# Products of zeros on TensorE in front of ten steps of the start of an attention and MLP kernel

## The chip, the cores and the metric

The kernel runs on one core of one Trainium2 chip. A core has TensorE (PE, matrix products into PSUM), VectorE (DVE), ScalarE (ACT), GpSimd (POOL) and SyncE (SP, which issues most DMAs). Each engine takes its own instructions strictly in order and waits on semaphores for the others. The metric is the device time of one execution in microseconds; lower is better.

## The reference

The inputs are q, k, v of shape (4, 8, 576, 64) in float32 and the weights of two dense blocks. What is computed, cut to what matters:

```python
q_d, k_d, v_d = (t.reshape(B, H, Sd, 4, D).mean(axis=3) for t in (q, k, v))
out_d = sm_attn(q_d, k_d, v_d)                       # softmax attention over 144 pooled positions
out_up = np.repeat(out_d, 4, axis=2)
mask = np.abs(pos[:, None] - pos[None, :]) < 4       # local attention, 7 keys wide
attn = softmax(np.where(mask, scale * q @ k.T, -1e9))
x = (out_up + attn @ v).transpose(0, 2, 1, 3).reshape(2304, 512)
x = ((x @ w_a) * (x @ w_b)) @ w_out                  # 512 -> 1536 -> 512
h = x @ w_in                                         # 512 -> 1024
solu = h * softmax(h)
out = layernorm(solu) * g_ln @ w_out2                # 1024 -> 512
```

## The kernel before, in words

The 2304 tokens are four batches of 576. The dense part works through five blocks of tokens (four of 512, one of 256). Each block runs through 12 chunks of the 1536 middle columns: `emit_A` makes the two products ab of a chunk (n = 0 for w_a, n = 1 for w_b), `emit_a` and `emit_mult` multiply them, `emit_p` splits the result into a high and a low part, and `emit_B` multiplies with w_out. Every float32 matrix is split into a high and a low part (xTh, xTl; a weight is a pair), and three products replace one. Weight tiles come through DMA as raw words; ACT (L109, L110), DVE (L114, L117), ACT (L123) and DVE (L130) turn each into such a pair.

Ahead of the first chunk the attention for the first 512 tokens has to be made. It has two parts, in small plain float32 products on TensorE.

- Pooled attention, for each of the four pairs of heads hp of batch 0: `qsum` (DVE L200, sums q and k over four positions into qkds), `scores` (PE L223, tile S), `smax` (DVE L233), `exps` (ACT L246, tile E), `norm` (DVE, POOL L255), `ptr` (PE transposes L266, tile PT), `pte` (ACT copy L272, PTs), `pvm` (PE L283, tile pv: 16 products of 144 columns), `pve` (ACT L289, tile up).
- Local attention, for each of the four strips s of 128 tokens: `scores` (PE L353, tile lS), `mask` (DVE L364, lP), `smax` (DVE L370, L371), `exps` (ACT L374), `norm` (DVE L380, POOL L383), `ptr` in two halves (PE transposes L393, tile lPT), `pte` (ACT copies L401, lPTs), `pvm` in two halves (PE L412, tile lo), `evac` (DVE L424, tile lx, adds up, which needs all four pairs), `split` (ACT L441 into xTh, then DVE or POOL L442 into xTl).

The first chunk then runs in halves of 256 columns: n = 0 and n = 1 on the first two strips, then n = 0 and n = 1 on the last two (L473, 12 products of 256 columns each). From the second chunk on, products have 512 columns.

The order on each engine is written out by hand: a table of times per step (L650 to L670) is sorted, the steps are emitted in that order, and no scheduler changes it. The SP queue is in the same table: the q and k tiles of the four pairs, the v tiles, then weight tiles and v strips by turns. ACT prepares weight tiles between attention steps: behind the copy of the first half of strip 0 stands L109 and L110 of its third weight tile, and behind these the copy L401 of strip 0's second half.

PSUM has two buffers tagged "ab" (PT, lPT of strips 0 and 1, then ab), acc0 and acc1 (S of odd pairs, lS of strip 2, later sums), x0 and x1 (pv, lo, lPT of strips 2 and 3, lS of strip 0 and from 4 on) and S.

A float32 product stands as two records in the profile's rows: the 16 products of pv are "x32" there. A transpose is one record, and so is a product of the split parts.

Of the kernel before, what the change touches and what calls it, by code (L numbers as in the profile page):

```python
# [7 lines left out]
F32 = mybir.dt.float32  # L8
# [20 lines left out]
EDGES = [8, 9, 13, 17]  # L29
NBOOT = NSUB  # L30
PT = [0, 16, 17]

QW, KW = 64, 70
TILES = [(t // 9, 64 * (t % 9), min(max(64 * (t % 9) - 3, 0), S - KW), 0, QW, 0) for t in range(NT // QW)]
# [4 lines left out]
def kernel(  # L39
# [98 lines left out]
    W1 = {}  # L138
    W2 = {}


    att = ExitStack()
    pool_p = att.enter_context(tc.tile_pool(name="pooled", bufs=1))
# [42 lines left out]
    def pooled_items(b, hp):  # L186
        i = b * NP + hp
        st = {}

        def room():  # L190

            if "room" not in st:
                st["room"] = slot(12 + hp, F32, (128, 1024), "E")
            return st["room"]

        def qsum(n):
            def f():
                if n == 0:
                    st["qk"] = pool_p.tile([128, 2, SD], F32, tag="qkds", name="qkds")
                DVE.tensor_reduce(out=st["qk"][:, n, :], in_=qkr[i][n].rearrange("p (c t) -> p c t", t=4),  # L200
                                  axis=AX.X, op=ALU.add)
            return f

        def vsum(kh):
            def f():
                if kh == 0:
                    st["v"] = pool_p.tile([72, 2, 2 * D], F32, tag="vds", name="vds")
                t = vr[i][:, kh, :].rearrange("p (t c) -> p t c", t=4)
                POOL.tensor_tensor(out=t[:, 0:2], in0=t[:, 0:2], in1=t[:, 2:4], op=ALU.add)
                POOL.tensor_tensor(out=st["v"][:, kh, :], in0=t[:, 0], in1=t[:, 1], op=ALU.add)  # L210
            return f

        def scores():
            if b:
                st["S"] = [aps.tile([72, 2 * SD], F32, tag=f"x{e}", name="S") for e in range(2)]
            elif hp % 2 == 0:
                t = aps.tile([72, 2, 512], F32, tag="S", name="S")
                st["S"] = [t[:, e, 0:2 * SD] for e in range(2)]
            else:
                st["S"] = [ps.tile([72, 512], F32, tag=f"acc{e}", name="S")[:, 0:2 * SD] for e in range(2)]  # L220
            for half in range(2):
                for e in range(2):
                    PE.matmul(  # L223
                        out=st["S"][e][:, half * SD:(half + 1) * SD],
                        lhsT=st["qk"][e * 64:e * 64 + 64, 0, half * 72:half * 72 + 72],
                        rhs=st["qk"][e * 64:e * 64 + 64, 1, :], start=True, stop=True,
                    )

        def smax():
            sv = [t.rearrange("p (h k) -> p h k", h=2) for t in st["S"]]  # L230
            mm = pool_p.tile([72, 2, 2], F32, tag="pm", bufs=2, name="pm")
            for e in range(2):
                DVE.tensor_reduce(out=mm[:, e, :], in_=sv[e], axis=AX.X, op=ALU.max)  # L233
            DVE.tensor_scalar(out=mm, in0=mm, scalar1=-scale / 16.0, scalar2=None, op0=ALU.mult)
            st["sv"], st["mm"] = sv, mm

        def exps():
            sv, mm = st["sv"], st["mm"]
            if b:
                st["E"] = pool_p.tile([72, 2, 2, SD], F32, tag="E", name="E")  # L240
            else:
                st["E"] = room()[:72, 0:4 * SD].rearrange("p (e h k) -> p e h k", e=2, h=2)
            st["ss"] = pool_p.tile([72, 4, 1], F32, tag="ss", bufs=2, name="ss")
            for e in range(2):
                for h in range(2):
                    ACT.activation(out=st["E"][:, e, h, :], in_=sv[e][:, h, :], func=AF.Exp,  # L246
                                   bias=mm[:, e, h:h + 1], scale=scale / 16.0,
                                   accum_out=st["ss"][:, 2 * e + h, :])

        def norm():  # L250
            ss = st["ss"].rearrange("p a o -> p (a o)")
            DVE.tensor_scalar(out=ss, in0=ss, scalar1=1e-9, scalar2=None, op0=ALU.add)
            DVE.reciprocal(out=ss, in_=ss)  # L253
            ev = st["E"].rearrange("p e h k -> p (e h) k")
            POOL.tensor_tensor(out=ev, in0=ev, in1=st["ss"].to_broadcast([72, 4, SD]), op=ALU.mult)  # L255

        def ptr():
            if b:
                st["PT"] = [aps.tile([72, 2 * SD], F32, tag=f"x{e}", name="PT") for e in range(2)]
            else:  # L260
                st["PT"] = [ps.tile([72, 512], F32, tag="ab", bufs=2, name="PT")[:, 0:2 * SD] for e in range(2)]
            for e in range(2):
                for kh in range(2):
                    for h in range(2):
                        o = kh * SD + h * 72
                        PE.transpose(st["PT"][e][:, o:o + 72], st["E"][:, e, h, kh * 72:kh * 72 + 72],  # L266
                                     id_sb[:72, :72])

        def pte():
            st["PTs"] = pool_p.tile([72, 2, 2, SD], F32, tag="PTs", name="PTs")  # L270
            for e in range(2):
                ACT.copy(out=st["PTs"][:, e].rearrange("p h k -> p (h k)"), in_=st["PT"][e])  # L272

        def pvm():
            st["pv"] = aps.tile([128, SD], F32, tag="x0", name="pv")
            if b:
                v = [st["v"][:, kh] for kh in range(2)]
            else:

                v = [vr[i][:, kh, 2 * D * t:2 * D * t + 2 * D] for kh in range(2) for t in range(4)]  # L280
            for n, vt in enumerate(v):
                for e in range(2):
                    PE.matmul(out=st["pv"][e * 64:e * 64 + 64, :], lhsT=vt[:, e * 64:e * 64 + 64],  # L283
                              rhs=st["PTs"][:, e, n * 2 // len(v), :], start=(n == 0), stop=(n == len(v) - 1))

        def pve():
            if b not in up:
                up[b] = pool_p.tile([128, NP, SD], F32, tag="up", bufs=2, name="up")
            ACT.activation(out=up[b][:, hp, :], in_=st["pv"], func=AF.Copy, scale=0.25)  # L289

        return dict(load=lambda: (load_qkr(i), load_v(i)), qsum0=qsum(0), qsum1=qsum(1), scores=scores,
                    vsum=lambda: (vsum(0)(), vsum(1)()), smax=smax, exps=exps, norm=norm, ptr=ptr, pte=pte,
                    pvm=pvm, pve=pve)

# [29 lines left out]
    def local_items(s):  # L324

        st = {}
# [13 lines left out]
        def scores(hps=range(NP)):  # L340
            if hps[0] == 0:
                if s in (1, 3):
                    t = aps.tile([128, 2, 512], F32, tag="S", name="lS")
                    st["S"] = [t[:, e] for e in range(2)]
                elif s == 2:
                    st["S"] = [ps.tile([128, 512], F32, tag=f"acc{e}", name="lS") for e in range(2)]
                else:
                    st["S"] = [aps.tile([128, 512], F32, tag=f"x{e}", name="lS") for e in range(2)]
            for hp in hps:
                for n in range(2):  # L350
                    for e in range(2):
                        q, k = qk_of(n, hp, e)
                        PE.matmul(out=st["S"][e][n * QW:n * QW + QW, hp * KW:hp * KW + KW], lhsT=q, rhs=k,  # L353
                                  start=True, stop=True, skip_group_check=True)
# [30 lines left out]
        def ptr(half):  # L385
            def f():
                if s < 2:
                    pt_ = ps.tile([KW, 4, 128], F32, tag="ab", bufs=2, name="lPT")
                else:
                    pt_ = aps.tile([KW, 4, 128], F32, tag=f"x{half}", name="lPT")  # L390
                for a in range(4):
                    hp, e = 2 * half + a // 2, a % 2
                    PE.transpose(pt_[:, a, :], st["P"][:, NP * e + hp, :], id_sb)  # L393
# [10 lines left out]
        def pvm(half):  # L404
            def f():
                if half == 0:
                    st["o"] = aps.tile([128, NP, 128], F32, tag="x1" if s < 2 else "x0", name="lo")
                for hp in (2 * half, 2 * half + 1):
                    for n in range(2):
                        for e in range(2):  # L410
# [49 lines left out]
    def emit_A(blk, j, n, c0, c1):  # L460

        xh, xl = xT_of(blk)
        if (blk, j) not in abs_:
            if width[blk] == WIDE:
                abs_[blk, j] = [ps.tile([128, WIDE], F32, tag="ab", bufs=2, name="ab") for _ in range(2)]
            else:
                t = ps.tile([128, 2, 256], F32, tag="ab", bufs=2, name="ab")
                abs_[blk, j] = [t[:, n_, :] for n_ in range(2)]
        wh, wl = W1[3 * j + n]
        for k in range(4):  # L470
            ws = slice(k * 128, k * 128 + 128)
# [247 lines left out]

    mhalf = base.tile([128, 1], F32, name="mhalf")  # L720
    DVE.memset(mhalf, -0.5)
    warm = base.tile([128, 1], F32, name="warm")
    ACT.activation(out=warm, in_=mhalf, func=AF.Exp)

# [145 lines left out]
```

## Time and profile before

| what | before |
|---|---|
| median of three runs | 805.21 us (800.87 to 806.71) |
| the profiled execution's own time | 803.08 us |
| its span, first to last instruction | 801.3 us |
| TensorE busy | 765.4 us (96%) |
| DVE, ACT, POOL busy | 376.9, 332.5, 228.5 us |
| chain of work that ended last | PE 81%, DVE 7%, ACT 5%, DMA 3% |
| largest chain lines | PE ab L473 33%, PE o L616 13%, PE h L548 11% |

The profile is of one execution. Rows of a timeline merge instructions of one kind that follow each other: start, length, engine, line, operation, output and inputs, count, and in brackets how long the engine stood idle before and what it waited for. "PEclk" is the clock that TensorE was granted, as a share of 2.4 GHz. The ends of products are modelled, so a row overlaps the start of the next by some hundredths of a microsecond. All times of rows count from the start of the span.

### The profile page before, as it was taken

To read this page: it belongs to the slowest core of one execution; us is meant where nothing else is said; L and a number is where in the kernel's file an instruction comes from. 1 tells how busy PE (TensorE), PEld (TensorE's weight loads), DVE (VectorE), ACT (ScalarE), POOL (GpSimd) and SP (SyncE) were. 2 spreads that over 40 slices of the span, in tenths; PEclk is the share of its full clock that TensorE was granted. 3 is DMA by queue.
4 is the path that set the end of the run, shared out by engine and by line. 5 is a ranking of instruction groups with operands and counts; after the bars stand their busy time and mean duration, and the time that the engine had idled before them with its cause. 6 is when DMAs were issued, how large, how long until landed. Compare 5 with 4: busy or idle time off the path is not lost.

```text
span 801.3 us, 12378 instructions
## 1 busy us (share of the span) xinstructions
PE 765.4 (96%) x4848; PEld 621.3 (78%) x4848; DVE 376.9 (47%) x689; ACT 332.5 (41%) x691; POOL 228.5 (29%) x204
## 2 busy tenths in 40 slices
PE   4979999998999999999999999999899999999997
PEld 3867777776787787777787888888788888888885
DVE  5678889974223324223213220126765373545441
ACT  3648777653222324322323221147645343344432
POOL 1242343431322222232111121114222352334320
PEclk9979999999999999999999999999999999999999
DMA  8977844214212203111102000036422554444321
GB/s 239 239 259 246 268 152 137 70 30 139 59 57 61 83 30 110 59 52 34 42 15 80 15 27 1 0 112 208 155 79 66 157 173 144 145 134 145 103 79 40
DMA packets 65226, 85.04 MB, mean 106 GB/s; under 512 B 9016, under 2 KB 46136, under 8 KB 65168
## 3 DMA queue, kind: packets, MB, share of 16 engines
q1 hardware_dynamic: 64864, 84.02, 33.8%
q8 instruction: 38, 0.62, 0.3%
q10 hardware_dynamic: 304, 0.23, 0.1%
q14 instruction: 20, 0.16, 0.1%
HBM read 66.93 MB, written 17.30 MB: 105 GB/s over the span
## 4 chain that ended last, share of the span: by engine, by line
PE 81%; DVE 7%; ACT 5%; DMA 3%; issue 3%; POOL 1%; SPq 0%; DVEq 0%; ACTq 0%; POOLq 0%
PE ab L473 33%; PE o L616 13%; PE h L548 11%; PE acc L507 8%; PE accS L507 7%; PE lo L412 2%; PE pv L283 2%; PE lPT L393 2%; DVE wm L117 2%; DMA qkr<-qkp 1%; PE lS L353 1%; PE S L223 1%; DMA raw<-w 1%; PE PT L266 1%; ACT o L514 1%
## 5 line engine op out<-in xcount | busy, mean ns | idle before, releaser
L473 PE MATMUL ab<-xTh,w 128*128 128x512 f32 (+1 forms) x976 | 298.0, 375 | 6.2 <-DVE a L483 3.6
L473 PEld LDWEIGHTS ab<-xTh,w 128*128 128x128 f32 x976 | 179.9, 191 | 43.7 <-DVE a L483 5.6
L473 PE MATMUL ab<-xTl,w 128*128 128x512 f32 (+1 forms) x488 | 180.2, 369 | 0.9 <-DVE xTl L167 0.5
L490 POOL TENSOR_TENSOR pl<-a,ph 128x512 fp32r<-128x512 f32 (+1 forms) x60 | 75.1, 1251 | 234.6 <-ACT ph L489 234.6
L483 DVE TENSOR_TENSOR a<-a,ab 128x512 f32<-128x512 f32 (+1 forms) x60 | 38.0, 632 | 181.3 <-PE ab L473 181.3
L473 PEld LDWEIGHTS ab<-xTl,w 128*128 128x128 f32 x488 | 93.4, 191 | 15.1 <-DVE xTl L167 0.9
L548 PE MATMUL h<-w,o1w 128*128 128x512 f32 x432 | 103.9, 391 | 1.1 <-ACT w L123 0.9
L548 PEld LDWEIGHTS h<-w,o1w 128*128 128x128 f32 x432 | 80.1, 188 | 18.1 <-ACT w L123 1.1
L616 PE MATMUL o<-w,cTh 128*128 128x512 f32 x288 | 91.0, 397 | 1.2 <-ACT cTh L606 0.9
L507 PE MATMUL acc<-ph,w 128*128 128x512 f32 (+1 forms) x288 | 90.2, 365 | 0.0
L478 ACT COPY a<-ab 128x512 f32<-128x512 f32 (+1 forms) x60 | 32.5, 542 | 108.9 <-PE ab L473 103.7
L507 PE MATMUL accS<-ph,w 128*128 128x512 f32 x192 | 68.0, 391 | 4.2 <-ACT o L514 4.2
L616 PEld LDWEIGHTS o<-w,cTh 128*128 128x128 f32 x288 | 54.0, 188 | 14.3 <-ACT cTh L606 1.1
L489 ACT CAST ph<-a 128x512 fp32r<-128x512 f32 (+1 forms) x60 | 34.6, 577 | 67.2 <-DVE a L483 67.2
L507 PEld LDWEIGHTS acc<-ph,w 128*128 128x128 f32 x288 | 52.2, 189 | 9.1 <-issue 1.2
L616 PE MATMUL o<-w,cTl 128*128 128x512 f32 x144 | 57.2, 397 | 0.1
L507 PE MATMUL acc<-pl,w 128*128 128x512 f32 (+1 forms) x144 | 51.1, 358 | 0.1
L600 POOL TENSOR_TENSOR cTl<-raw,cTh 128x1024 fp32r<-128x1024 f32 x15 | 36.0, 2401 | 44.2 <-ACT cTh L599 36.6
L507 PEld LDWEIGHTS accS<-ph,w 128*128 128x128 f32 x192 | 36.0, 188 | 13.1 <-ACT o L514 5.5
L117 DVE CUSTOM_DVE_ANT_0 wm<-raw,wm 128x1024 uint16<-128x1024 uint16 x52 | 43.4, 845 | 2.3
L255 POOL TENSOR_TENSOR E<-E,ss 72x576 f32<-72x576 f32 x16 | 19.3, 1206 | 81.1 <-DVE ss L253 53.4
L557 DVE TENSOR_REDUCE mx<-h 128x1 f32<-128x1024 f32 x18 | 22.0, 1223 | 43.1 <-PE h L548 43.1
(91 smaller groups left out, 1005.5 us busy)
## 6 DMA issues: line engine op xcount, KB each, us to landing
raw<-w SPq DMA_DIRECT2D x52, 512.0 KB
qkr<-qkp SPq DMA_DIRECT2D x32, 288.0 KB
vd<-v SPq DMA_DIRECT2D x15, 512.0 KB
raw<-vd SPq DMA_DIRECT2D x60, 128.0 KB
vw<-vwin SPq DMA_DIRECT2D x36, 140.0 KB
vp<-vp SPq DMA_DIRECT2D x16, 288.0 KB
o1r<-o1d SPq DMA_DIRECT2D x18, 256.0 KB
out<-ob SPq DMA_DIRECT2D x18, 256.0 KB
```

What stands on the lines that cost most here:

```text
L117: DVE.tensor_tensor(out=st["w"], in0=st["w"], in1=st["low"], op=ALU.add)
L255: POOL.tensor_tensor(out=ev, in0=ev, in1=st["ss"].to_broadcast([72, 4, SD]), op=ALU.mult)
L473: PE.matmul(out=abs_[blk, j][n][:, c0:c1], lhsT=w[:, ws], rhs=x[:, k, c0:c1], start=(k == 0 and i == 0), stop=(k == 3 and i == 2), skip_gr ...
L478: ACT.copy(out=a, in_=abs_[blk, j][0])
L483: DVE.tensor_tensor(out=a, in0=a, in1=pb, op=ALU.mult)
L489: ACT.copy(out=ph, in_=a)
L490: POOL.tensor_tensor(out=pl, in0=a, in1=f32(ph), op=ALU.subtract)
L507: PE.matmul(out=accs[blk][m], lhsT=wt[:, ms], rhs=x, start=(j == 0 and i == 0 and (w == WIDE or m % 2 == 0)), stop=(j == NCH - 1 and i == ...
L548: PE.matmul(out=h[:, n * 512:n * 512 + 512], lhsT=x[:, ks], rhs=w, start=(k == 0 and q_ == 0), stop=(k == 3 and q_ == 2))
L557: DVE.tensor_reduce(out=mx, in_=st["h"], axis=AX.X, op=ALU.max)
L600: POOL.tensor_tensor(out=h4(lo), in0=raw, in1=f32(h4(hi)), op=ALU.subtract)
L616: PE.matmul(out=o, lhsT=x[:, k, :], rhs=w, start=(k == 0 and q_ == 0), stop=(k == 7 and q_ == 2))
```

## The change

A tile `zz` of 128 by 128 zeros is made by POOL at the start. A new helper `fill(key, out)` issues as many products of zeros by zeros on TensorE as the table `FILL` has under that key, 72 in all. They write into a part of the PSUM tile that the step behind them is about to use (before it does), or into a tile `fz` on acc1. Calls stand ahead of the scores, the transposes, the lo products and the first ab of a block; only the ten keys of the table have products.

```diff
--- before.py
+++ after.py
@@ -29,6 +29,8 @@
 EDGES = [8, 9, 13, 17]
 NBOOT = NSUB
 PT = [0, 16, 17]
+
+FILL = dict(lS0_0=12, lS0_1=9, lS0_3=6, PT0=5, S3=7, lPT0_0=6, lo1_0=10, lPT2_1=6, A0_256=7, lS4_0=4)
 
 QW, KW = 64, 70
 TILES = [(t // 9, 64 * (t % 9), min(max(64 * (t % 9) - 3, 0), S - KW), 0, QW, 0) for t in range(NT // QW)]
@@ -138,6 +140,18 @@
     W1 = {}
     W2 = {}
 
+    zz = base.tile([128, 128], F32, name="zz")
+
+    fz = []
+
+    def fill(key, out):
+        for _ in range(FILL.get(key, 0)):
+            if out is None:
+                if not fz:
+                    fz.append(ps.tile([128, 512], F32, tag="acc1", name="fz"))
+                out = fz[0][:, 0:128]
+            PE.matmul(out=out, lhsT=zz[:, 0:out.shape[0]], rhs=zz, start=True, stop=True, skip_group_check=True)
+
 
     att = ExitStack()
     pool_p = att.enter_context(tc.tile_pool(name="pooled", bufs=1))
@@ -218,6 +232,8 @@
                 st["S"] = [t[:, e, 0:2 * SD] for e in range(2)]
             else:
                 st["S"] = [ps.tile([72, 512], F32, tag=f"acc{e}", name="S")[:, 0:2 * SD] for e in range(2)]
+            if not b:
+                fill(f"S{hp}", st["S"][0][:, 0:128])
             for half in range(2):
                 for e in range(2):
                     PE.matmul(
@@ -259,6 +275,8 @@
                 st["PT"] = [aps.tile([72, 2 * SD], F32, tag=f"x{e}", name="PT") for e in range(2)]
             else:
                 st["PT"] = [ps.tile([72, 512], F32, tag="ab", bufs=2, name="PT")[:, 0:2 * SD] for e in range(2)]
+            if not b:
+                fill(f"PT{hp}", st["PT"][0][:, 0:128])
             for e in range(2):
                 for kh in range(2):
                     for h in range(2):
@@ -346,6 +364,7 @@
                     st["S"] = [ps.tile([128, 512], F32, tag=f"acc{e}", name="lS") for e in range(2)]
                 else:
                     st["S"] = [aps.tile([128, 512], F32, tag=f"x{e}", name="lS") for e in range(2)]
+            fill(f"lS{s}_{hps[0]}", None if s > 3 else st["S"][1][:, 384:512])
             for hp in hps:
                 for n in range(2):
                     for e in range(2):
@@ -388,6 +407,7 @@
                     pt_ = ps.tile([KW, 4, 128], F32, tag="ab", bufs=2, name="lPT")
                 else:
                     pt_ = aps.tile([KW, 4, 128], F32, tag=f"x{half}", name="lPT")
+                fill(f"lPT{s}_{half}", None if s > 1 else pt_[:, 0, :])
                 for a in range(4):
                     hp, e = 2 * half + a // 2, a % 2
                     PE.transpose(pt_[:, a, :], st["P"][:, NP * e + hp, :], id_sb)
@@ -405,6 +425,7 @@
             def f():
                 if half == 0:
                     st["o"] = aps.tile([128, NP, 128], F32, tag="x1" if s < 2 else "x0", name="lo")
+                fill(f"lo{s}_{half}", None)
                 for hp in (2 * half, 2 * half + 1):
                     for n in range(2):
                         for e in range(2):
@@ -466,6 +487,8 @@
             else:
                 t = ps.tile([128, 2, 256], F32, tag="ab", bufs=2, name="ab")
                 abs_[blk, j] = [t[:, n_, :] for n_ in range(2)]
+        if (blk, j) == (0, 0):
+            fill(f"A{n}_{c0}", None)
         wh, wl = W1[3 * j + n]
         for k in range(4):
             ws = slice(k * 128, k * 128 + 128)
@@ -719,6 +742,7 @@
 
     mhalf = base.tile([128, 1], F32, name="mhalf")
     DVE.memset(mhalf, -0.5)
+    POOL.memset(zz, 0.0)
     warm = base.tile([128, 1], F32, name="warm")
     ACT.activation(out=warm, in_=mhalf, func=AF.Exp)
 
```

Each key is a step: lS0_0, lS0_1 and lS0_3 are the scores of strip 0 for pairs 0, 1 and 3; PT0 the transposes of pair 0; S3 the pooled scores of pair 3; lPT0_0 the first half of strip 0's transposes; lo1_0 the lo products of strip 1; lPT2_1 the second half of strip 2's transposes; A0_256 the first product of the first chunk on the last two strips; lS4_0 the scores of strip 4, which belongs to the next block.

TensorE's order, from its first instruction to the pooled scores of pair 3. Before:

```order
L353 MATMUL lS<-qkr 64x70 x4
L223 MATMUL S<-qkds 72x144 x4
L353 MATMUL lS<-qkr 64x70 x4
L223 MATMUL S<-qkds 72x144 x4
L353 MATMUL lS<-qkr 64x70 x8
L223 MATMUL S<-qkds 72x144 x4
L266 MATMUL PT<-id_sb,E 72x72 x8
L223 MATMUL S<-qkds 72x144 x4
L283 MATMUL pv<-PTs,vp 64x144 x16
```

After (line numbers are those of the changed file):

```order
L153 MATMUL lS<-zz 128x128 x12
L372 MATMUL lS<-qkr 64x70 x4
L239 MATMUL S<-qkds 72x144 x4
L153 MATMUL lS<-zz 128x128 x9
L372 MATMUL lS<-qkr 64x70 x4
L239 MATMUL S<-qkds 72x144 x4
L372 MATMUL lS<-qkr 64x70 x4
L153 MATMUL lS<-zz 128x128 x6
L372 MATMUL lS<-qkr 64x70 x4
L239 MATMUL S<-qkds 72x144 x4
L153 MATMUL PT<-zz 72x128 x5
L284 MATMUL PT<-id_sb,E 72x72 x8
```

Behind the last of these rows come seven products of zeros, then the scores S of pair 3. Nothing of before has changed its place against its neighbours.

TensorE's order further on, from the scores of strip 3 to the lo products of strip 2. Before:

```order
L353 MATMUL lS<-qkr 64x70 x16
L393 MATMUL lPT<-id_sb,lP 70x128 x4
L283 MATMUL pv<-PTs,vp 64x144 x16
L393 MATMUL lPT<-id_sb,lP 70x128 x4
L266 MATMUL PT<-id_sb,E 72x72 x8
L412 MATMUL lo<-lPTs,vw 64x64 x8
L393 MATMUL lPT<-id_sb,lP 70x128 x8
L412 MATMUL lo<-lPTs,vw 64x64 x8
L283 MATMUL pv<-PTs,vp 64x144 x16
L412 MATMUL lo<-lPTs,vw 64x64 x16
L393 MATMUL lPT<-id_sb,lP 70x128 x8
L412 MATMUL lo<-lPTs,vw 64x64 x16
```

After, from the first half of strip 0's transposes:

```order
L153 MATMUL lPT<-zz 70x128 x6
L413 MATMUL lPT<-id_sb,lP 70x128 x4
L301 MATMUL pv<-PTs,vp 64x144 x16
L413 MATMUL lPT<-id_sb,lP 70x128 x4
L284 MATMUL PT<-id_sb,E 72x72 x8
L433 MATMUL lo<-lPTs,vw 64x64 x8
L413 MATMUL lPT<-id_sb,lP 70x128 x8
L433 MATMUL lo<-lPTs,vw 64x64 x8
L301 MATMUL pv<-PTs,vp 64x144 x16
L153 MATMUL fz<-zz 128x128 x10
L433 MATMUL lo<-lPTs,vw 64x64 x16
L413 MATMUL lPT<-id_sb,lP 70x128 x4
```

Behind that come six products of zeros, the other four transposes of strip 2 and its lo products. Between the six ahead of lPT and the ten behind pv of pair 3 none is added. The orders of DVE, ACT and SP are as before; POOL's has one row more, the memset of zz, ahead of its first use by the attention.

## Rows read from the trace of the kernel before

**Rows 1.** Busy time by stretch: start:end length, engines, PEclk, DMA share, GB/s

```profile
20.00:27.60 7.60, 7.60 (x109) 6.87 (x107) 2.16 (x6) 3.74 (x12) 0.27 (x1) 1.00 0.94 216
27.80:41.30 13.50, 11.33 (x188) 9.56 (x184) 12.73 (x25) 10.04 (x21) 5.01 (x5) 1.00 0.95 251
41.40:51.50 10.10, 8.37 (x83) 7.12 (x84) 8.88 (x14) 5.68 (x10) 5.14 (x4) 0.50 0.71 260
51.70:58.30 6.60, 4.72 (x61) 4.28 (x60) 3.24 (x5) 2.81 (x5) 3.14 (x5) 1.00 0.65 232
58.50:61.80 3.30, 3.30 (x18) 2.71 (x18) 2.30 (x7) 0.62 (x1) 0.00 (x0) 0.50 1.03 416
64.60:801.30 736.70, 718.80 (x4280) 582.50 (x4280) 333.75 (x605) 299.70 (x602) 211.96 (x185) 1.00 0.30 93
```

**Rows 2.** Timeline of TensorE, 13 to 34 us

```profile
13.31 0.51 PE L353 MATMUL lS<-qkr 64*64 64x70 f32 x8 [1.40 <-DMA qkr<-qkp]
13.76 1.24 PE L223 MATMUL S<-qkds 64*72 64x144 f32 x8
...
19.38 4.40 PE L283 MATMUL pv<-PTs,vp 72*64 72x144 f32 x32 [1.53 <-ACT PTs L272]
23.71 1.18 PE L266 MATMUL PT<-id_sb,E 72*72 72x72 f32 x8
24.82 2.15 PE L353 MATMUL lS<-qkr 64*64 64x70 f32 x64
26.90 2.55 PE L283 MATMUL pv<-PTs,vp 72*64 72x144 f32 x32
29.38 0.69 PE L266 MATMUL PT<-id_sb,E 72*72 72x72 f32 x8
30.00 0.72 PE L353 MATMUL lS<-qkr 64*64 64x70 f32 x32
31.49 0.63 PE L393 MATMUL lPT<-id_sb,lP 128*70 128x128 f32 x4 [0.77 <-POOL lP L383]
32.05 2.18 PE L283 MATMUL pv<-PTs,vp 72*64 72x144 f32 x32
```

**Rows 3.** Timeline of ACT around its third weight tile

```profile
33.17 0.71 ACT L109 ACTIVATE raw<-raw 128x512 f32<-128x512 f32 x1 [0.43 <-DMA raw<-w]
...
34.83 0.58 ACT L401 COPY lPTs<-lPT 70x512 f32<-70x512 f32 x1 [0.37 <-PE lPT L393]
```

**Rows 4.** Timeline of TensorE, 35 to 85 us

```profile
35.46 0.45 PE L266 MATMUL PT<-id_sb,E 72*72 72x72 f32 x4 [0.42 <-ACT lPTs L401]
...
36.46 1.07 PE L393 MATMUL lPT<-id_sb,lP 128*70 128x128 f32 x8
...
38.21 2.18 PE L283 MATMUL pv<-PTs,vp 72*64 72x144 f32 x32
42.98 1.97 PE L412 MATMUL lo<-lPTs,vw 70*64 70x64 f32 x32 [2.58 <-DVE lx L424]
...
54.11 1.15 PE L412 MATMUL lo<-lPTs,vw 70*64 70x64 f32 x32
56.71 0.39 PE L473 MATMUL ab<-xTh,w 128*128 128x256 f32 x1 [1.45 <-ACT xTh L441]
...
84.88 0.71 PE L223 MATMUL S<-qkds 64*72 64x144 f32 x8
```

**Rows 5.** Chain of work that ended last, in order of time, 42 to 70 us

```profile
42.32 0.61 DVE lx L424
...
49.15 2.73 PE ab L473 x12
...
52.75 1.43 PE ab L473 x12
...
57.53 1.96 PE ab L473 x11
...
64.61 5.74 PE ab L473 x24
```

## The prediction, before the changed kernel was run

> **What bounds the kernel now.** I read the views in this order: granted clock and busy time by stretch, the PE, ACT and DVE timelines of the first 65 us with what ended each wait, and the chain of work that ended last. From 64.6 us on TensorE is busy for 718.80 of 736.70 us [rows 1], and a chain row there starts the second chunk at 64.61 [rows 5]. So what the change gains or loses by 64.61 is what the kernel gains or loses, and all else is about those 65 us.
>
> There the reader is to see two things. First, the clock. The row for 20 to 27.6 us says 1.00, but the 32 pv records at 19.38 took 4.40 us and the same 32 at 32.05 took 2.18 [rows 2]: TensorE ran at 1.2 GHz until about 27.7, and the record of the clock just starts later. After that it is 2.4 GHz to 41.3, 1.2 to 51.5, 2.4 to 58.3, 1.2 to 61.8, then 2.4 [rows 1]. Second, in this stretch TensorE is often not what ends the wait: at 13.31 it waited for q and k, at 31.49 for POOL, at 35.46 for an ACT copy, at 42.98 for DVE, at 56.71 for ACT [rows 2, 4].
>
> **The change, part by part.** It adds one memset on POOL, ahead of anything that POOL is waited for, and 72 products of 128 by 128 zeros in TensorE's order; all other rows of all engines keep their order. No f32 product over the whole array stands in the trace. From below: pv makes 16 products of 144 columns in 2.18 us, 0.136 each, so 0.12 for 128 columns. From above: pv fills half of the array's columns with each product and two can run side by side, so 0.24 alone. I take 0.23 at 2.4 GHz, since a zero product fills the array, and 0.46 at 1.2.
>
> *Up to 13.31 us* 27 zero products run where TensorE waits for q and k; hidden. If the clock is at 2.4 GHz from there on, this becomes shorter on TensorE: S 1.24 to 0.71 (0.53) [rows 2, 4], pv of pair 0 4.40 to 2.18 (2.22), PT 1.18 to 0.69 (0.49), 64 lS records 2.15 to twice 0.72 (0.71), pv of pair 1 2.55 to 2.18 (0.37) [rows 2]: 4.3 us. Against it stand 18 zero products: five ahead of the first PT (in what the shorter S leaves), seven ahead of S3 (1.6 us against the 1.53 that pv waited at 19.38), six ahead of lPT (1.4 against 0.77): 0.5 us. TensorE comes to 35.04 about 3.8 us early.
>
> *This doesn't pass.* ACT's third L109 started at 33.17, after 0.43 us of waiting for its weight tile to land [rows 3]. Nothing in the change touches the SP queue, so it starts then again, and everything behind it in ACT's order waits. The copy L401 behind it had waited 0.37 for TensorE at 34.83: it comes 0.37 earlier, and that is the whole gain at this gate. The transposes PT of pair 3 wait for this copy (35.46, 0.42 idle) [rows 4], so they start at 35.09, and TensorE's idle time ahead of them grows to 0.42 + 3.8 - 0.37 = **3.85 us**. None of the zero products stands in this hole.
>
> *What the clock does there.* Before both falls in the trace TensorE had stood idle for less: the fall at 41.3 came about a microsecond into the 2.58 us ahead of lo at 42.98, and that at 58.4 right after 1.45 us ahead of ab at 56.71 and 0.43 more behind it (56.71 + 0.39 to 57.53) [rows 1, 4, 5]. So I take it to fall in the hole. It did not rise during the 4.40 us of pv at 19.38, which had no gap [rows 2]; PT, lo, lPT, lo and pv, which come after the hole, are work of that kind. At 2.4 GHz they took from 35.46 to 40.39 (0.45, the lo, 1.07, lo, 2.18) [rows 4]. At 1.2: half of 1.18, half of 1.97, twice 1.07, half of 1.97, 4.40, together 9.1, less 0.3 for overlapping ends: 8.8, so to 43.9. DVE's lx (42.32 before [rows 5]) needs that pv and moves too.
>
> *The ten zero products behind pv*, which would fill the 2.58 us wait, now start at 43.9 and cost between 2.3 (clock up at once) and 4.6; I take 4.0, for the clock comes up late: 47.9. Then lo 1.15 [rows 4], 49.05; lx 0.61 [rows 5], beside it half an lPT (0.55) and six zero products (1.4), 51.0; the other half 0.55, L401 0.58 [rows 3], half of lo 0.58: 52.7. Before, this point was 49.15: **3.55 late**. From here on the clock is at 2.4: ab 2.73 to 1.43 (1.30 back); then from 51.88 to 57.53 copies, transposes and lo as before, 5.6 us, with seven zero products in the 1.45 + 0.43 of waiting; the next ab 1.96 for 11 to 1.31 (0.65 back) [rows 5], S 1.24 to 0.71 (0.53 back). The wait behind that is DVE and ACT work of the same length. Four zero products (0.9) lie beside it. Sum: 3.55 - 1.30 - 0.65 - 0.53 = +1.1.
>
> The profiled execution took 803.08 us, so **804.1**, I say 804. With the ten at 2.3 it is 802.4, at 4.6 it is 804.8. The median of the runs shown is 2.1 above the profiled one, so the time can come out that much higher.
>
> If every slow piece on the path came back whole, it would be 4.3 and, further on, 0.82 (lo, 1.97 to 1.15), 1.30, 0.65, 0.53: 7.6 us. The Trainium skill (TensorE: Matmul & The Clock Gate, Part 1) says that the cost of coming up to the full clock is under 1% of a typical kernel's span, here 8.0 us: by that bound too, a gain of over 1% is all but out, though for this kernel rows and page come close to it.
>
> **Rivals.**
> *The clock holds through the hole*, or comes up too late for the hole to open. For it: gaps of 0.42 and 0.77 us did no harm in 27.8 to 41.3 [rows 1, 2, 4]. Against: 3.85 is longer than the gaps at both falls. Then 0.37 (gate), 0.82 (lo ahead of 49.15), 1.30, 0.65 and 0.53 all come back: 3.7, **799.4**.
> *The gate is none*: the tile lands earlier, and 7.6 comes back: **795.5**. Against: L109 waited for this landing, with the DMA share at 0.95 around it [rows 1, 3].
> *Zero products don't bring the clock up.* Each costs 0.46. The 18 ahead of the gate take 8.3 us against 0.53 + 1.53 + 0.77 of waits, 5.5 late, of which 0.4 is hidden by ACT's wait; the ten 4.6 against 2.58 (2.0), the seven 3.2 against 1.9 (1.3); of the six (2.8) and the four (1.8) I take 0.7 as hidden, since no wait of that length stands there (3.9). That is 12.3 late: **815.4**. It decides from 0.26 us a product on, where ten outlast 2.58 us. For it: no row shows a product of zeros. Against: the rows show nothing by which values matter. The Trainium skill (same page, Part 1) has the clock gate watch how busy the engine is, and names zeros only for another limiter, one that needs three busy cores; no run here shows either.
> *A second fall* further on, in the waits at 56 or 60, adds up to 2 us to the forecast: 806.
>
> **How the numbers follow.** The hole and its fall: 0.48 (802.4 to 804.8). The clock holds: 0.36 (799.4). Zeros don't count: 0.07. No gate: 0.05. A second fall: 0.04. The likeliest gives 804. The range takes in the first two and the last, and the 2.1 between profile and median: 798.5 to 807, which leaves out the 0.12 of the outer two and some of the spread. About 1% is what a measurement of this kernel can tell from no change, 8 us: faster by that needs the missing gate, 0.04; slower needs zeros that don't count, 0.07; the rest, 0.89, lies within.
>
> **What would show it.** In the changed profile: pv of pair 0 takes 2.2 us (if 4.4, the clock did not rise). ACT's third L109 still starts near 33.2, now with about 4 us of idle ahead. TensorE idles 3 to 4 us ahead of PT of pair 3, and pv behind it takes 4.4 (if 2.2, the clock held and the time is near 799). The ten zero products take 2.3 to 4.6. The first ab starts near 52.7, or near 48 by the first rival. The forecast is wrong if the third weight tile lands earlier or if the clock reads 2.4 GHz from 28 us on.

## The result, and the profile after

The changed kernel takes 799.84 us (median of 20 executions, 795.28 to 805.80), the kernel before 807.56 beside it (20, 800.73 to 812.54): ratio 0.992, interval 0.989 to 0.995. That is a gain of 0.8%, inside the 1% within which the prediction called a difference none, and the median lies inside the predicted range, 4 us below the predicted 804. The two profiled executions, 803.08 and 799.16 us, differ by 3.9, the medians by 7.7. This factor of two is the subject of much of what follows. The ratio is worked out from the executions of both kernels and is not the ratio of the two medians.

Of the profile after, busy time by stretch (start:end length, PE, PEld, DVE, ACT, POOL, PEclk, DMA share, GB/s), which answers to [rows 1]:

```profile
5.00:30.00 25.00, 23.88 (x361) 20.35 (x360) 20.08 (x45) 12.40 (x47) 6.74 (x6) 1.00 0.97 284
31.40:44.80 13.40, 13.05 (x98) 11.54 (x100) 8.05 (x16) 6.90 (x15) 3.42 (x3) 0.50 0.89 255
45.00:64.00 19.00, 18.10 (x238) 16.45 (x235) 12.30 (x23) 11.01 (x25) 5.90 (x7) 1.00 0.62 227
```

Of the timeline of TensorE after, the rows that answer to [rows 2, 4] (start, length, line, operation, output and inputs, count, and in brackets the idle time ahead with what ended it; L153 is the line of the zero products, each of which leaves two records):

```profile
0.99 4.34 PE L153 MATMUL lS<-zz 128*128 128x128 f32 x24 [0.99 <-POOL zz L745]
...
11.57 0.35 PE L372 MATMUL lS<-qkr 64*64 64x70 f32 x8
...
16.95 2.47 PE L301 MATMUL pv<-PTs,vp 72*64 72x144 f32 x32 [0.23 <-ACT PTs L290]
...
26.70 2.18 PE L301 MATMUL pv<-PTs,vp 72*64 72x144 f32 x32
...
31.75 0.69 PE L284 MATMUL PT<-id_sb,E 72*72 72x72 f32 x4 [2.05 <-ACT lPTs L421]
...
36.19 4.05 PE L301 MATMUL pv<-PTs,vp 72*64 72x144 f32 x32
40.17 4.64 PE L153 MATMUL fz<-zz 128*128 128x128 f32 x20
...
49.63 0.39 PE L496 MATMUL ab<-xTh,w 128*128 128x256 f32 x1
...
63.10 0.50 PE L496 MATMUL ab<-xTh,w 128*128 128x512 f32 x1 [0.40 <-ACT a L501]
```

And of ACT's timeline after, the third weight tile, which answers to [rows 3] (L111 was L109):

```profile
30.02 0.67 ACT L111 ACTIVATE raw<-raw 128x512 f32<-128x512 f32 x1 [2.62 <-DMA raw<-w]
```

The reader is to see the forecast's chain in it. The zeros bring the clock up early (pv of pair 0 takes 2.47, not 4.40). By pv of pair 2 TensorE is 5.35 us early (26.70 against 32.05); 1.74 of that is there already at lS of pair 3 (11.57 against 13.31), because q and k landed earlier in this execution, and 3.61 is what the zeros bring. ACT then waits 2.62 us for the third weight tile, TensorE stands idle for 2.05 behind it, and the clock falls to 1.2 GHz from 31.2 to 44.9. In that stretch pv of pair 3 takes 4.05 and the ten zeros 4.64. What is not as forecast is the place of it all: the tile landed 3.15 us earlier than in the profile of before. The second chunk starts at 63.10, 1.51 ahead of before [rows 5], instead of 1.1 behind it.

### The profile page after: what moved, and what is told of

Read it like the earlier page. It is cut to its first block, busy times and chain, and to the rows that moved or that the text cites. A ratio compares the mean times of both kernels' runs of the same rounds, so it can differ in the third digit from the quotient of the medians.

```text
span 797.4 us, 12666 instructions
## 1 busy us (share of the span) xinstructions
PE 775.4 (97%) x4992; PEld 633.4 (79%) x4992; DVE 374.9 (47%) x689; ACT 332.0 (42%) x691; POOL 229.5 (29%) x205
## 4 chain that ended last, share of the span: by engine, by line
PE 79%; DVE 7%; DMA 5%; ACT 4%; issue 4%; POOL 1%; SPq 0%; DVEq 0%; ACTq 0%; POOLq 0%
PE ab L496 32%; PE o L639 13%; PE h L571 10%; PE acc L530 8%; PE accS L530 7%; PE lo L433 2%; PE lPT L413 2%; DMA vw<-vwin 2%; DVE wm L119 2%; PE pv L301 1%; DMA raw<-w 1%; DMA qkr<-qkp 1%; DVE wm L116 1%; PE lS L372 1%; PE fz L153 1%
## 5 line engine op out<-in xcount | busy, mean ns | idle before, releaser
L496 PEld LDWEIGHTS ab<-xTh,w 128*128 128x128 f32 x976 | 177.8, 189 | 41.5 <-DVE a L506 5.8
L119 DVE CUSTOM_DVE_ANT_0 wm<-raw,wm 128x1024 uint16<-128x1024 uint16 x52 | 41.6, 810 | 2.3
```

Source lines behind the costliest of these rows:

```text
L119: DVE.tensor_tensor(out=st["w"], in0=st["w"], in1=st["low"], op=ALU.add)
L496: PE.matmul(out=abs_[blk, j][n][:, c0:c1], lhsT=w[:, ws], rhs=x[:, k, c0:c1], start=(k == 0 and i == 0), stop=(k == 3 and i == 2), skip_gr ...
```

## The experiments

Each kernel was timed beside the kernel before. That kernel's medians there were 807.31 (first four rows below), 803.96 (the next four) and 806.0 (the last two).

| kernel | zeros | median us (range, executions) | ratio [95%] |
|---|---|---|---|
| e1_early | the six places ahead of 27 us (45) | 798.45 (795.72 to 802.67, 10) | 0.992 [0.989, 0.996] |
| e2_late | the four places behind it (27) | 799.66 (796.94 to 809.29, 12) | 0.994 [0.990, 0.997] |
| e3_hole | all 72, and ten in the hole | 795.18 (794.07 to 797.35, 6) | 0.988 [0.983, 0.992] |
| e4_swap | all 72; the tile that ACT prepares third is loaded earlier | 796.10 (795.42 to 798.98, 6) | 0.989 [0.985, 0.994] |
| b2_before | none: before, unchanged | 808.36 (1) | |
| e5_swap_before | none; the loads as in e4 | 808.60 (801.05 to 811.62, 12) | 1.003 [0.999, 1.006] |
| e6_swap_hole | all 72, ten in the hole, loads as in e4 | 794.84 (794.49 to 795.58, 6) | 0.988 [0.983, 0.992] |
| e7_first27 | the first three places alone (27) | 805.82 (799.04 to 811.55, 12) | 1.000 [0.996, 1.003] |
| e8_mid | the fourth to sixth place alone (18) | 798.54 (795.61 to 802.47, 12) | 0.992 [0.988, 0.995] |
| a2_after | all 72: the change, unchanged | 801.63 (795.79 to 807.71, 12) | 0.994 [0.990, 0.998] |

**Two halves of the change.** The first splits it at the gate on ACT, the second keeps what the first leaves out.

```diff
-FILL = dict(lS0_0=12, lS0_1=9, lS0_3=6, PT0=5, S3=7, lPT0_0=6, lo1_0=10, lPT2_1=6, A0_256=7, lS4_0=4)
+FILL = dict(lS0_0=12, lS0_1=9, lS0_3=6, PT0=5, S3=7, lPT0_0=6)          # e1_early
+FILL = dict(lo1_0=10, lPT2_1=6, A0_256=7, lS4_0=4)                      # e2_late
```

> Only the 45 products of zeros up to the first transposes of strip 0 (keys lS0_0, lS0_1, lS0_3, PT0, S3, lPT0_0); the 27 behind the hole are left out. My theory (the early gain stops at ACT's third weight tile, TensorE stands idle there, the clock falls, and it is the later zeros that bring it back): pv of pair 0 near 2.2 to 2.5 us, ACT's third L109 with 2 to 4 us of idle ahead of it, pv of pair 3 at 4 us or more, both lo of strips 1 and 2 near 1.97 and the first ab near 2.7, the second chunk between 64 and 66.5 us; ratio to before 0.998 to 1.003. Rival 1 (the gain is pv of pair 0 and what else is early): ratio near 0.992, second chunk near 62.

> Only the 27 products of zeros from 40 us on (keys lo1_0, lPT2_1, A0_256, lS4_0). My theory: the start is as before, so no hole at the third weight tile and pv of pair 3 at 2.2 us; the ten zeros behind it keep the clock at 2.4 GHz, lo 1.15 for 1.97, first ab 1.43 for 2.73, second ab and S at full clock: second chunk near 61.3 instead of 64.6, ratio 0.992 to 0.996, as good as the change or better. Rival 1: without the early zeros nothing is gained, ratio 1.00. Rival 2 (one place of ten is too little to hold the clock): ten zeros at 4.6 us, lo later than before, ratio 1.000 to 1.003.

The early half alone gives what the whole gives, 0.992, where 0.998 to 1.003 was expected; its rival came. In e1's profile the clock does not fall in the hole:

```profile
32.51 0.44 PE L284 MATMUL PT<-id_sb,E 72*72 72x72 f32 x4 [0.94 <-ACT lPTs L421]
...
35.27 2.18 PE L301 MATMUL pv<-PTs,vp 72*64 72x144 f32 x32
...
61.43 0.50 PE L496 MATMUL ab<-xTh,w 128*128 128x512 f32 x1 [0.40 <-ACT a L501]
```

It falls at about 40 us, behind the wait for DVE that the ten late zeros would have filled.

The late half alone has two groups of times: eight executions at 796.9 to 801.7, four at 805.6 to 809.3. Its profile fell into the second group (805.61), not into the case that was expected (second chunk near 61.3). TensorE in it:

```profile
25.41 4.11 PE L301 MATMUL pv<-PTs,vp 72*64 72x144 f32 x32
...
42.92 4.05 PE L301 MATMUL pv<-PTs,vp 72*64 72x144 f32 x32
46.90 3.73 PE L153 MATMUL fz<-zz 128*128 128x128 f32 x20
50.56 1.15 PE L433 MATMUL lo<-lPTs,vw 70*64 70x64 f32 x32
...
68.87 0.50 PE L496 MATMUL ab<-xTh,w 128*128 128x512 f32 x1 [0.40 <-ACT a L501]
```

Here the clock stayed at 1.2 GHz from the start until the ten zeros brought it up (lo behind them takes 1.15, at 1.2 GHz it takes 1.97), and the second chunk starts 4.26 us later than in the profile of before. Nothing in the edit makes the first 40 us slower, so the kernel before had to be looked at again.

**The kernel before once more**, with a second profile.

> The kernel before, unchanged, profiled once more. Its 21 timed executions fall into two groups that don't overlap in mean granted clock: 799 to 805 us at 0.983 to 0.993 and 807 to 810 at 0.995 to 0.998. My theory now: the record of the clock starts with its first change, so a high mean beside a long time is an execution whose clock stayed at 1.2 GHz, unrecorded, until about 50 us. If this execution takes 807 us or more: pv of all four pairs at 4.1 to 4.4 us, PT of pair 3 near 38, second chunk near 68 to 70. If it takes under 805: pv of pair 2 near 2.2 as in the first profile, second chunk near 64. Rival (the slow group loses its time later, in the dense part): second chunk near 64.6 in either group.

It took 808.36 us. Its TensorE (L283 is pv, L473 ab), and its busy time from 20 to 58 us:

```profile
17.47 4.40 PE L283 MATMUL pv<-PTs,vp 72*64 72x144 f32 x32 [1.25 <-ACT PTs L272]
...
24.98 4.11 PE L283 MATMUL pv<-PTs,vp 72*64 72x144 f32 x32
...
32.26 4.11 PE L283 MATMUL pv<-PTs,vp 72*64 72x144 f32 x32
...
42.48 4.05 PE L283 MATMUL pv<-PTs,vp 72*64 72x144 f32 x32
...
69.32 0.50 PE L473 MATMUL ab<-xTh,w 128*128 128x512 f32 x1 [0.40 <-ACT a L478]
```

```profile
20.00:58.00 38.00, 36.55 (x371) 30.99 (x368) 24.59 (x43) 18.31 (x37) 12.47 (x11) 1.00 0.69 195
```

All four pv take 4.05 to 4.40: the clock stays at 1.2 GHz until 58 us, though the row of the clock says 1.00, since its record begins with the first change. The second chunk starts at 69.32 against 64.61 [rows 5]: 4.7 us, and the profiled executions differ by 5.3.

So the kernel before has two kinds of executions: the clock rises at about 28 us, as in the profile that the prediction read, or much later, at 58 in this profile. Every execution has its mean recorded clock, and this tells the kinds apart, the wrong way round for the reason just given. One execution of each kind was profiled; the others are sorted by time and mean clock alone. Of the 23 executions beside e8 and a2, ten took 799.65 to 803.86 us with a mean of 0.987 to 0.990, and thirteen 805.37 to 811.40 with 0.995 to 0.999. In the 22 beside e5 to e7 it was thirteen at 800.45 to 804.26 and nine at 805.81 to 811.23; in the 21 beside e1 to e4 nine at 801.67 to 805.14, eleven at 807.31 to 811.40, and one at 799.20 (0.993) that fits neither. The median is that of a mixture, and moves with the share of the kinds.

**Ten zeros in the hole; the gate moved.** Two ways to keep the clock up past the forecast's hole: fill it, or move the gate. The weight tile that ACT prepares third (wst[3] below) is the fourth in SP's order; the swap loads it in the third one's place, so that no copy waits behind a tile that has just been asked for.

```diff
-FILL = dict(..., lPT0_0=6, lo1_0=10, ...)
+FILL = dict(..., lPT0_0=6, PT3=10, lo1_0=10, ...)                       # e3_hole

-... locs[1]["loadv"], wst[2][0], locs[2]["loadv"], locs[3]["loadv"]] + [wst[i][0] for i in range(3, 6)]
+... locs[1]["loadv"], wst[3][0], locs[2]["loadv"], locs[3]["loadv"]] + [wst[i][0] for i in (2, 4, 5)]   # e4_swap
```

> The change, and ten more products of zeros ahead of the transposes of pair 3 (key PT3), inside the hole at the third weight tile. My theory: TensorE's idle time there falls from 2.05 us to under 0.5, the granted clock stays at 2.4 GHz from about 4 us on, pv of pair 3 takes 2.2 us (4.05 with the change), the ten zeros behind it 2.3 (4.64), the second chunk starts near 60.5 (63.10 with the change): ratio to before 0.986 to 0.989. Rival: the clock is not what makes pv of pair 3 slow, or the wait is moved only: ratio as with the change, 0.992.

> The change, and the loads of weight tiles 2 and 3 trade places on SP's queue, so that the third tile that ACT asks for (number 3) is loaded two places of v strips earlier. My theory (this landing is the gate): ACT's third L109 has no wait, TensorE's idle time ahead of the transposes of pair 3 falls under 0.7 us, the second chunk starts 3 us or more earlier than with the change, near 60: ratio to before 0.985 to 0.989. Rival (the gate is the order of ACT's work, or the next tile lands too late as well): the wait moves to the fourth tile, ratio as with the change, 0.992.

In the profiles of both the clock is up at pv of pair 3. TensorE and ACT's third tile of e3, then of e4:

```profile
32.66 2.35 PE L153 MATMUL PT<-zz 128*72 128x128 f32 x20
...
37.92 2.18 PE L301 MATMUL pv<-PTs,vp 72*64 72x144 f32 x32 [0.18 <-ACT up L307]
```

```profile
30.55 0.70 ACT L111 ACTIVATE raw<-raw 128x512 f32<-128x512 f32 x1
```

```profile
32.18 0.44 PE L284 MATMUL PT<-id_sb,E 72*72 72x72 f32 x4 [0.42 <-ACT lPTs L421]
...
34.94 2.18 PE L301 MATMUL pv<-PTs,vp 72*64 72x144 f32 x32
...
58.46 0.50 PE L496 MATMUL ab<-xTh,w 128*128 128x512 f32 x1 [0.40 <-ACT a L501]
```

```profile
27.61 0.67 ACT L111 ACTIVATE raw<-raw 128x512 f32<-128x512 f32 x1
```

In both, pv of pair 3 takes 2.18, not 4.05. In e4 ACT's third tile has no wait at all, and the second chunk starts at 58.46, 4.64 us ahead of the change. e3's profile is no test of the ten zeros: its clock fell at about 12 us and came back at about 15.5, TensorE was late, and ACT's third tile had no wait there either, so there was no hole to fill; the second chunk starts at 61.44 (60.5 was expected). The executions are the test. No execution of either kernel takes over 799.0 us, where of the change's first twenty thirteen take 799.16 to 805.80: what they take away is the upper part of the change's spread, and the medians fall to 795.18 and 796.10. All twelve executions of the two have a mean clock of 0.995 or more, against 14 of the change's 32 (below). (The ratios, 0.988 and 0.989 against 0.992, have intervals that overlap; the spreads tell more.)

**Each edit without the other, and both.** The swap on the kernel before, which has no zeros; and the swap with the ten in the hole.

```diff
# e5_swap_before: only the two lines of e4's swap, on the kernel before
# e6_swap_hole: e4's swap and PT3=10 on the change
```

> The kernel before, without any product of zeros, and the loads of weight tiles 2 and 3 trade places on SP's queue. My theory: without the zeros TensorE is late itself (ACT waited 0.43 us for the third tile), so an earlier landing frees at most that: ratio 0.997 to 1.001. Rival (the landing is what limits the kernel before too): second chunk 2 us or more earlier, ratio 0.994 or less.

> The change, with both the ten zeros ahead of the transposes of pair 3 and the loads of weight tiles 2 and 3 traded. My theory: each alone already holds the clock at 2.4 GHz through the hole (0.9876 and 0.9892), together there is nothing left to wait for: 0.984 to 0.988, second chunk near 59 to 60, no fall of the clock ahead of it. Rival: the ten zeros now stand on the path, since the tile is early, and cost up to 2 us: 0.989 to 0.991.

Without zeros the swap gives nothing (1.003, interval 0.999 to 1.006). e5's median is 4.6 us above the 803.96 beside it, but that is the share of the kinds: four of its twelve executions are of the kind that rises early (801.05 to 803.83), thirteen of the 22 there. In its profile (802.07) ACT's third tile has no wait:

```profile
31.66 0.70 ACT L109 ACTIVATE raw<-raw 128x512 f32<-128x512 f32 x1
```

TensorE still waits 0.42 us ahead of the second half of PT of pair 3, as before: it is late enough that the third tile isn't what it waits for. The gate binds only once the zeros make TensorE early, as the prediction said. With both, 794.84: no better than e3 (the two intervals are all but the same). TensorE in e6 runs the ten zeros at 30.63, without a wait behind them, and starts the second chunk at 59.39, 0.93 later than e4. It reached lS of pair 3 1.01 later too (12.90 against 11.89), so the two profiles do not show that zeros in a closed hole cost time:

```profile
30.63 2.35 PE L153 MATMUL PT<-zz 128*72 128x128 f32 x20
...
59.39 0.50 PE L496 MATMUL ab<-xTh,w 128*128 128x512 f32 x1 [0.40 <-ACT a L501]
```

Its six executions lie within 1.1 us, the narrowest of all, and no kernel here measurably beats it.

**Which of the early zeros do it.**

```diff
+FILL = dict(lS0_0=12, lS0_1=9, lS0_3=6)                                 # e7_first27
+FILL = dict(PT0=5, S3=7, lPT0_0=6)                                      # e8_mid
```

> Only the 27 products of zeros that lie in the waits for q and k (keys lS0_0, lS0_1, lS0_3). My theory (what the early zeros buy is that the clock is up before pv of pair 0 in every execution instead of late or not at all): the clock rises near 5 us, the slow group of the kernel before is gone, ratio 0.992 to 0.997. Rival (the zeros around the transposes and S3 are needed to hold it): the clock falls again near 14 to 18 us, pv of pair 0 at 4.4 us, ratio 0.997 to 1.000.

> Only the 18 products of zeros ahead of the first PT, of S3 and of the first lPT (keys PT0, S3, lPT0_0), none in the waits for q and k. My theory (what counts is that TensorE has dense full-array work right ahead of pv of pair 0, not how early it starts): the twelve zeros from 14 us on run at 1.2 GHz, 0.37 us each as the first twelve did in the change, and make pv of pair 0 about 2 to 3 us late, but the clock rises near 18 to 22 us in every execution; the delay is hidden behind the third weight tile; no slow group at 807 or more; ratio 0.992 to 0.997. Rival 1 (the 27 zeros ahead are needed to bring it up): the clock stays low, the delay of 3 us remains, ratio 1.000 to 1.004.

The first 27, which the prediction let bring the clock up, give nothing alone: 1.000, where 0.992 to 0.997 was expected; the rival came. Five of e7's executions take 799.04 to 802.56 us (mean clock 0.982 to 0.985), seven 805.05 to 811.55 (0.966 to 0.977). In the profiled one, the longest of the twelve (811.55), the zeros bring the clock up and it is lost again; the others have no profile. Busy time by stretch, and TensorE:

```profile
5.00:11.30 6.30, 4.83 (x56) 3.87 (x54) 3.25 (x7) 0.19 (x1) 0.00 (x0) 1.00 0.97 331
11.50:62.50 51.00, 46.43 (x439) 39.27 (x440) 32.17 (x64) 25.11 (x71) 14.72 (x12) 0.50 0.69 188
```

```profile
12.13 0.51 PE L372 MATMUL lS<-qkr 64*64 64x70 f32 x8 [1.28 <-DMA qkr<-qkp]
12.57 2.93 PE L153 MATMUL lS<-zz 128*128 128x128 f32 x12
...
22.00 4.40 PE L301 MATMUL pv<-PTs,vp 72*64 72x144 f32 x32 [1.54 <-ACT PTs L290]
```

The clock rises at 4.6 us and falls at 11.4, beside the waits for q and k; six zeros behind it, 2.93 us at 1.2 GHz, don't bring it back, and it stays low to 62.6. The 18 of e8, twelve of them ahead of pv of pair 0 and six ahead of lPT, alone give 0.992, as much as all 72. e8's TensorE and its stretches:

```profile
16.50 1.73 PE L153 MATMUL S<-zz 128*72 128x128 f32 x14
18.80 2.18 PE L301 MATMUL pv<-PTs,vp 72*64 72x144 f32 x32
...
39.21 1.15 PE L433 MATMUL lo<-lPTs,vw 70*64 70x64 f32 x32 [2.48 <-DVE lx L445]
...
61.23 0.50 PE L496 MATMUL ab<-xTh,w 128*128 128x512 f32 x1 [0.40 <-ACT a L501]
```

```profile
16.70:40.40 23.70, 20.39 (x364) 17.75 (x362) 19.48 (x39) 16.26 (x45) 6.75 (x7) 1.00 0.99 249
40.60:50.60 10.00, 8.91 (x64) 7.59 (x62) 7.24 (x10) 5.50 (x10) 7.21 (x7) 0.50 0.59 222
```

The clock rises at 16.7, eleven microseconds before the earlier kind of the kernel before, and falls at 40.5 behind the 2.48 us wait that the ten late zeros would have filled, as before at 41.3 [rows 1].

**The change once more**, to see whether its own profile shows all of it.

> The change, unchanged, profiled and timed once more beside it. My theory (in each execution the clock either falls in the hole at the third weight tile or holds): its executions lie between 795 and 806 us, those with a mean granted clock of 0.995 and more below 799.5 and those under 0.992 above; if this profile holds the clock from 6 us on, pv of pair 3 takes 2.2 us and the second chunk starts near 60 to 61; if it falls at 31 to 36 us, pv takes 4 us and the second chunk starts near 63. Rival: time and granted clock don't go together.

It does not. TensorE of this second profile (800.80 us), and ACT's third tile:

```profile
31.27 2.17 PE L301 MATMUL pv<-PTs,vp 72*64 72x144 f32 x30 [1.88 <-issue]
...
35.14 0.45 PE L284 MATMUL PT<-id_sb,E 72*72 72x72 f32 x4 [0.89 <-ACT lPTs L421]
...
37.89 2.18 PE L301 MATMUL pv<-PTs,vp 72*64 72x144 f32 x32
40.00 2.50 PE L153 MATMUL fz<-zz 128*128 128x128 f32 x20
...
61.40 0.50 PE L496 MATMUL ab<-xTh,w 128*128 128x512 f32 x1 [0.40 <-ACT a L501]
```

```profile
33.40 0.68 ACT L111 ACTIVATE raw<-raw 128x512 f32<-128x512 f32 x1 [3.77 <-DMA raw<-w]
```

The tile lands at 33.40, as the prediction took it, and ACT waits 3.77 us for it. But the idle time of TensorE is split, 1.88 us inside pv of pair 2 and 0.89 ahead of PT, and the clock holds: pv of pair 3 takes 2.18. So both of the prediction's main cases happen, each in one of the two profiled executions of the same kernel. (Why the 1.88 and the 0.89 let the clock stay up and the 2.05 did not was not tried.) Of these twelve, six have a mean clock of 0.997 or more and take 795.79 to 800.80 us; the other six have 0.990 or less and take 802.46 to 807.71. Of the change's first 20, the eight with 0.995 or more take 795.28 to 799.19, the twelve others 799.16 to 805.80. (Here a low mean is a fall, as it should be, since the clock rises and its record begins within the first microseconds. It does not say where the fall lies: a2's 0.998 has one from 597.1 to 600.4, PEclk 0.50, and none in the hole. Nine of the first 20 lie between 0.990 and 0.997, where none of a2's twelve does, so the cut at 0.995 sorts them only roughly.)

## Why the prediction was right, and where its steps failed

**Right: early gain, stopped at the gate, given back by a fall.** Each step is in the profile of the change. The early gain came to 3.61 us. The recorded sum has 3.8, from 4.3 less 0.5; its own terms, 1.6 against 1.53 and 1.4 against 0.77, add up to 0.7, and this gives 3.6. The fall has the price that the sum gave it: from the second half of PT of pair 3 to the second chunk it is 31.35 us in the change's profile, which falls (31.75 to 63.10), and 26.26 in a2, which holds (35.14 to 61.40), 5.1 apart, where the two cases, 804.1 and 799.4, are 4.7 apart. In e1's profile, which holds through the hole without the late zeros, the stretch is 28.92, so they bring 2.7 there; the medians (798.45 in e1, 799.84 and 801.63 in the change) don't show this gain, and why stays open. e3 and e4, which fill the hole or take away what makes it, have no execution above 799.0 us. e5 fits the gate: without the zeros an earlier tile gives nothing. The step "to 52.7" holds when counted from the gate: the first ab came at 49.63, and the tile 3.15 us earlier than the 33.17 that the sum began with; 49.63 + 3.15 is 52.78.

**Failed: one profile of before was taken for the kernel.** The sum was made against 803.08 us, in which the clock rose by itself at 27.7. In about half of the executions, by time and mean clock, it rises much later. There the zeros bring much more: from lS of pair 3 to the end of pv of pair 2 it is 25.0 us in b2, 20.9 in the first profile of before and 17.3 in the change, so 7.7 instead of 3.6. The prediction saw that the median stood 2.1 above its profile and put it down as a shift of the whole; it was the sign of a second kind, and the change takes that kind away: the longest times of before, 810 to 812 us, don't occur in any kernel with zeros at PT0, S3 and lPT0_0. So the sum has the wrong sign: it gave 1.1 us more, and the medians fell by 7.7. That the forecast stands all the same is partly luck: "no difference" reached 8 us either way, and the range of 8.5 us took in the median of a mixture that the prediction had not seen.

**Failed: the gate at 33.17.** "Nothing in the change touches the SP queue, so it starts then again": the queue's order was the same, its times were not. Where ACT waited for this tile, it started at 33.17 in the first profile of before, at 30.02 and 33.40 in two of the change, at 30.76 in e1 and 30.02 in e8. In b2 it started at 32.85 with no wait, so the tile had landed by then:

```profile
32.85 0.68 ACT L109 ACTIVATE raw<-raw 128x512 f32<-128x512 f32 x1
```

Most of the spread is there when SP issues the load, the first of three in these rows, before and then after:

```profile
26.18 1.50 SPq L101 DMA_DIRECT2D raw<-w  x3
```

```profile
23.35 1.33 SPq L103 DMA_DIRECT2D raw<-w  x3
```

b2 issues it at 22.96, a2 at 25.71. The first profile of before and a2 are late from the first v tile on (7.64 and 7.59, against 5.81 in b2 and 5.62 in the change's first profile), behind a wait of 2.0 and 1.9 us on SP that the profile puts down to the load of mk_sb. One profile of each kernel is late and one early, so nothing here ties this to the change; what makes it stays open. A gate read from one execution has a spread of more than 3 us, which alone is three times the +1.1 that the sum ended with. The hole was 2.05, not 3.85, since the gate came earlier by more than TensorE did.

**Mis-stated: the fall as a case of the kernel.** It was given 0.48 and the clock that holds 0.36, as alternatives. They are shares of the executions: by the mean clock, 12 and 8 of the first 20, 6 and 6 of the next 12 (one of each kind was profiled). The holding ones have medians of 796.7 and 797.7 us (799.4 was worked out for that case), the falling ones 802.2 and 803.6 (804). The prediction's two cases are thus the two kinds, each put 0.4 to 2.7 us too high, and the median of the mixture lies between them.

**Put at nothing: the spread behind 64.6 us.** The change's first profile is 1.51 ahead at the second chunk and 3.77 at the last matrix product. Part of that shows at the start of the second block, at about 190 us, in a wait of TensorE for ACT; before, with the stretch behind it, then a2:

```profile
190.34 0.50 PE L507 MATMUL accS<-ph,w 128*128 128x512 f32 x1 [2.49 <-ACT o L514]
...
191.60:194.90 3.30, 3.30 (x31) 2.58 (x24) 2.28 (x4) 0.59 (x2) 0.00 (x0) 0.50 1.09 316
```

```profile
188.14 0.50 PE L530 MATMUL accS<-ph,w 128*128 128x512 f32 x1 [2.59 <-ACT o L537]
```

Before waits 2.49 us and its clock falls for 3.3. The change's first profile waits 1.94 and its clock doesn't fall; but a2 waits 2.59 and b2 2.28, and theirs doesn't fall there either. From the start of the second chunk to the end of the span it is 736.7 and 737.3 us in the two profiles of before, 734.3 and 737.6 in the two of the change. So these two or three microseconds differ between executions of one kernel, and no run ties them to the change; the sum had no term for them.

**Sizes.** A zero product costs 0.25 us at 2.4 GHz (ten in 2.50, a2) and 0.46 at 1.2 (ten in 4.64); 0.23 and 0.46 were taken. That zeros might not bring the clock up is refuted by e8. The Trainium skill (TensorE: Matmul & The Clock Gate, Part 1) puts the cost of coming up to the full clock at under 1% of a typical kernel's span. Here e3, which adds nothing but zeros, takes 1.2% off (interval 0.8 to 1.7%), and this counts later falls as well as the rise; the interval takes in 1%, so no run here contradicts the page.

## What to carry to other kernels

Before summing terms of a microsecond from one profile, look at the spread of the executions: two groups of times with two mean clocks are like two kernels, and a change may act on one of them alone. Filler products pay where they bring the clock up for good, and a gap that the time so won opens behind the next load may need filler too, or the load moved; here 18 products did as much as 72, and with ten more in the one new hole none of six executions took as long as those that fell back. Whether products of other values, or of smaller shape, would do as well wasn't tried. A landing read from one trace is a sample: give it its spread before a forecast rests on it.

## What the runs showed of the hardware

- At the start of the program TensorE may stay at 1.2 GHz to about 28 us or to about 58, with the same instructions. pv products without a gap (4.11 us twice in the second profile of before, at 24.98 and 32.26) did not end this; zeros over the whole array did, within 3.73 us in e2's profile. What decides between the two stays open.
- A mean clock near 1.00 can stand for a stretch that ran at 1.2 GHz, as the stretch of 20 to 58 us above, while its record has not begun. The length of a known product (pv: 2.18 or 4.1 to 4.4) tells the clock.
- In a2, e4 and e1, TensorE stood still for 1.88, 1.29 and 0.51 us behind the first product of pv of pair 2, with no wait that the profile shows. Its cause wasn't tried.
